# Second mixture: two arms behind 256 unbranched columns instead of seven widths, and one copy of the last tile's halves per expert

## The chip, the core and the metric

The kernel runs on one core of one Trainium2 chip. The metric is the device time of one execution in microseconds (us), lower is better. The core has five engines that run their own instruction streams and wait for each other through semaphores: TensorE (PE; its weight loads are shown apart as PEld), VectorE (DVE), ScalarE (ACT), GpSimd (POOL) and SyncE (SP), which issues most of the DMA transfers. SBUF is the working memory, PSUM the memory into which TensorE writes its products.

## The reference, cut to what matters

Attention without a softmax feeds a dense block, and that feeds a mixture of eight experts ("the second mixture"), which is the part that the change touches. Each of 2,304 tokens goes to one expert; an expert takes at most `capacity` = 576 tokens.

```python
for i in range(N):                       # N = 2304
    e = expert_idx[i]
    if counts[e] < capacity:             # capacity = 576
        disp[e, counts[e]] = x[i]
        pos[i] = counts[e]; counts[e] += 1; keep[i] = True
h = np.maximum(np.einsum('ecd,edf->ecf', disp, w1), 0.0)   # 512 -> 1024, per expert
y = np.einsum('ecf,efd->ecd', h, w2)                       # 1024 -> 512
for i in range(N):
    if keep[i]:
        out[i] = gate_w[i] * y[expert_idx[i], pos[i]]
```

With the input of this case the experts are handled in an order that gives token counts of 625 (cut to 576), 167, 219, 614 (cut to 576), 160, 391, 76 and 52. The numbers can't be known when the program is built: the kernel reads them into registers and branches on them.

## The kernel before

Every f32 operand is split into a high and a low half (type f32r), and a product of two such operands is made of three products on TensorE (`PASSES`). For one expert the first matrix, w1, is taken in eight slices `f` of 128 rows of the hidden layer (`NF2` = 8). `part(e, f, h, o, w)` is one slice over `w` token columns: 12 products (4 chunks of the depth by 3 passes) into one PSUM tile. `hb` holds three such tiles of two banks each, and slice `f` uses tile `(8e + f) % 3`, so a slice waits for the readers of the third slice before it. `put_g` reads the tile over all 576 columns, whatever the expert's count is: ACT writes the high half of the rectified value to `g2[f][:, 0]`, then DVE the low half to `g2[f][:, 1]`.

How many columns TensorE computes is chosen on the chip: `widths` is a tree of branches on TensorE alone, with seven arms, 256, 304, 352, 400, 448, 512 and 576 columns (`LEVELS`). Each arm has its own code, so slice `f` holds 6 x 12 + 24 = 96 products in its program, of which 12 or 24 run. All experts but the first are unrolled in this way: `up2(e, i)` holds two slices, under a branch of all engines on whether the expert has over 128 tokens. An expert with at most 128 takes the other side of that branch, `turned`, where the tokens are the stationary operand: 12 products of 256 columns for two slices, a copy by ACT, and two transposes.

A slice of 576 columns does not fit in one bank, so that arm starts in the middle of the first bank, and ACT and DVE read from a register offset, `off[e]`, which is 0 or 256.

After the up part comes `down(e, t)`, one tile of 128 tokens at a time: `whole` with three passes, or, for a tile with at most 64 tokens, `half`, whose stationary operand `gl` holds high and low halves of 64 tokens side by side. `gl[f]` is copied out of `g2[f]` on ACT by `put_last`, once for each slice, at the column `last[e]`.

The instructions of each engine run in the order in which the program is written (`manual_schedule`). Around the up part ACT and POOL also split the weights that come in by DMA (`next_pair`: two casts on ACT, two subtractions on POOL for each pair of tiles), ten pairs ahead of their use. A pair's stage buffer is one of four; SP issues the next load when POOL has released one, and the loads of the next expert's tokens (`load_x`, tile `xr`) stand in the same queue.

Of the kernel before, what the change touches and what calls it, by code (L numbers as in the profile page):

```python
# [19 lines left out]
P = 128  # L20
# [6 lines left out]
def attn_moe_kernel(ctx: ExitStack, tc: tile.TileContext, cap, kp, vp, qt, gn, wm, wg, wgt, w1, w2, ident, tri, out):  # L27
# [28 lines left out]
    tri_sb = const.tile([P, 2, P], BF16, name="tri_sb")  # L56
    cnt = const.tile([P, E], F32, name="cnt")
    cnt_i = const.tile([P, E], I32, name="cnt_i")
    off_i = const.tile([P, E], I32, name="off_i")
    last_i = const.tile([P, E], I32, name="last_i")  # L60

    ek_i = const.tile([P, E], I32, name="ek_i")
# [460 lines left out]

    LAG, LEAD = 2, 4
    HOT = 9
    LEVELS = (NARROW, 304, 352, 400, 448, BANK, cap)
    units = []

    with tc.manual_schedule(engines={mybir.EngineType.SP}):
# [189 lines left out]
        v.tensor_scalar(cnt, cnt, 1.0, -1.0, op0=ALU.max, op1=ALU.add)  # L719
        v.tensor_copy(last_i, cnt)  # L720
        v.tensor_scalar(last_i, last_i, 7, 7, op0=ALU.logical_shift_right, op1=ALU.logical_shift_left)
        v.tensor_scalar(off_i, cnt, float(BANK - 1), float(BANK - NARROW), op0=ALU.is_gt, op1=ALU.mult)
    ph1.close()


# [7 lines left out]
    psum = [ctx.enter_context(tc.tile_pool(name=f"psum{i}", bufs=1, space=PSUM)) for i in range(2)]  # L733
    hb = [psum[0].tile([P, 2 * BANK], F32, name=f"hb{i}") for i in range(3)]
    bk = [psum[1].tile([P, 512], F32, name=f"bk{i}") for i in range(2)]
    g2 = [g2_p.tile([P, 2, cap], F32R, name=f"g2_{f}") for f in range(NF2)]

    gl = [g2_p.tile([P, 2, HALF], F32R, name=f"gl_{f}") for f in range(NF2)]
    x2 = x2_p.tile([P, 2, KD, cap], F32R, name="x2")
    meta = {}  # L740

# [16 lines left out]
    with tc.manual_schedule():  # L758
# [44 lines left out]
        def part(e, f, h, o, w, x=x2):  # L803


            order = [(c, a, m) for c in range(KD) for a, m in PASSES]
            if f == 0:
                order = [(c, a, m) for a, m in ((0, 0), (1, 0), (0, 1)) for c in range(KD)]
            for k, (c, a, m) in enumerate(order):
                nc.tensor.matmul(  # L810
                    h, lhsT=w1_at(e, f // 2, a, c)[:, f % 2 * P:(f % 2 + 1) * P], rhs=x[:, m, c, o:o + w],
                    start=k == 0, stop=k == 3 * KD - 1,
                )

        def widths(e, levels, arm):

            mid = len(levels) // 2
            if not mid:
                return arm(levels[0])
            with tc.If(n[e] > levels[mid - 1]) as c:  # L820
                widths(e, levels[mid:], arm)
            with c.Else():
                widths(e, levels[:mid], arm)

        def up(e, f):

            h = hb[(e * NF2 + f) % 3]

            def arm(w):
                if w > BANK:  # L830
                    part(e, f, h[:, BANK - NARROW:BANK], 0, NARROW)
                    part(e, f, h[:, BANK:BANK + w - NARROW], NARROW, w - NARROW)
                else:
                    part(e, f, h[:, :w], 0, w)

            widths(e, LEVELS, arm)
            put_g(f, h[:, bass.ds(off[e], cap)], slice(0, cap))

        turned_sb = [ht_p.tile([P, 2 * P], F32, name=f"turned{i}") for i in range(2)]

# [10 lines left out]
        def up2(e, i):  # L851

            with tc.If(nall[e] > P) as many:  # L853
                up(e, 2 * i)
                up(e, 2 * i + 1)
            with many.Else():
                if i == 0:
                    nc.scalar.copy(turned_sb[0], turned(e, 0))
                if i + 1 < NF2 // 2:
                    s = turned(e, i + 1)  # L860
                hs = [hb[(e * NF2 + 2 * i + k) % 3][:, :P] for k in range(2)]
                for k, h in enumerate(hs):
                    nc.tensor.transpose(h, turned_sb[i % 2][:, k * P:(k + 1) * P], id_sb)
                if i + 1 < NF2 // 2:
                    nc.scalar.copy(turned_sb[(i + 1) % 2], s)
                for k, h in enumerate(hs):
                    put_g(2 * i + k, h, slice(0, P))
            for f in range(2 * i, 2 * i + 2):
                put_last(f, bass.ds(last[e], HALF))

        def put_g(f, src, cols):

            g = g2[f][:, :, cols]
            nc.scalar.activation(out=g[:, 0], in_=src, func=AF.Relu)  # L874
            nc.vector.scalar_tensor_tensor(  # L875
                out=g[:, 1], in0=src, scalar=0.0, in1=f32(g[:, 0]), op0=ALU.max, op1=ALU.subtract
            )

        def put_last(f, cols):
            nc.scalar.copy(gl[f], f32(g2[f][:, :, cols]))  # L880

        def up_rest(f):

            h = hb[f % 3][:, BANK:]
            with tc.If(n[0] > BANK) as wide:
                part(0, f, h[:, :cap - NARROW], NARROW, cap - NARROW)
            with wide.Else():
                with tc.If(n[0] > NARROW) as some:
                    part(0, f, h[:, :BANK - NARROW], NARROW, BANK - NARROW)
                with some.Else():  # L890
                    nothing(h, P)
            put_g(f, h[:, :cap - NARROW], slice(NARROW, cap))
            put_last(f, bass.ds(last[0], HALF))

        def down(e, t):
            w = rows(t)

            ps = hb[((e + 1) * NF2 + t + (e + 1 < E)) % 3][:, :BANK] if t < 2 else bk[t % 2]

            m = meta[e]  # L900
            o = ypool.tile([P, ROW], F32, tag="y", name="o")

            def products(lhs, passes):
                k, n = lhs(0, 0).shape[1], 0
                for f in range(NF2):
                    for a, b in passes:
                        nc.tensor.matmul(  # L907
                            ps[:k, :], lhsT=lhs(f, a), rhs=we2[e, f][:, b, :],
                            start=n == 0, stop=n == len(passes) * NF2 - 1,
                        )  # L910
                        n += 1

            def whole():
                products(lambda f, a: g2[f][:, a, t * P:t * P + w], PASSES)
                nc.scalar.activation(out=o[:w, :DM], in_=ps[:w, :], func=AF.Copy, scale=m[:w, t, 0:1])
                scatter("out", out, m[:w, t, 1:2].bitcast(I32), o[:w, :DM], NTOK - 1)

            def half():

                products(lambda f, a: gl[f].rearrange("p a t -> p (a t)"), ((0, 0), (0, 1)))  # L920
                g = m[:HALF, t, 0:1]
                nc.scalar.activation(out=o[:HALF, :DM], in_=ps[:HALF, :], func=AF.Copy, scale=g)  # L922
                nc.vector.scalar_tensor_tensor(  # L923
                    out=o[:HALF, :DM], in0=ps[HALF:, :], scalar=g, in1=o[:HALF, :DM], op0=ALU.mult, op1=ALU.add
                )
                scatter("out", out, m[:HALF, t, 1:2].bitcast(I32), o[:HALF, :DM], NTOK - 1)

            if w <= HALF:
                half()
            else:  # L930
                with tc.If(nall[e] > t * P + HALF) as more:  # L931
                    whole()
                with more.Else():
                    half()
# [17 lines left out]
        for f in range(3):  # L952
# [13 lines left out]
            skip_runtime_bounds_check_because="the counts are clamped to the capacity on the chip",  # L966
        )

        _, off = nc.values_load_multi_w_load_instructions(
            off_i[0:1, :], engines=[ET.Activation, ET.DVE], min_val=0, max_val=BANK - NARROW,  # L970
            skip_runtime_bounds_check_because="the offsets are one of two numbers",
        )

        _, last = nc.values_load_multi_w_load_instructions(
            last_i[0:1, :], engines=[ET.Activation], min_val=0, max_val=(cap - 1) // P * P,
            skip_runtime_bounds_check_because="the counts are clamped to the capacity on the chip",
# [11 lines left out]
        for e in range(E):  # L988
            if e + 1 < E:
                for t in range(4):  # L990
                    load_x(e + 1, t)
            if e == 0:
                with tc.If(early > NARROW - 1) as done:
                    for f in range(NF2):
                        up_rest(f)
                with done.Else():
                    tr_x(0, 0)
                    tr_x(0, 1)
                    for f in range(NF2):
                        up(0, f)  # L1000
                        put_last(f, bass.ds(last[0], HALF))
            else:
                for i in range(NF2 // 2):
                    up2(e, i)
                    if i < NF2 // 2 - 1:
                        next_pair((AP, AP))
            if e + 1 < E:
                tr_x(e + 1, 0)
                tr_x(e + 1, 1)
                for t in range(4, NST):  # L1010
                    load_x(e + 1, t)
            if e:
                next_pair((AP, AP))
            next_pair((AP, AP))
            next_pair((AP, AP))
            down(e, 0)
            if e + 1 < E:
                rest_x(e + 1, range(2, NST))
            with tc.If(nall[e] > P) as some:  # L1019
                down(e, 1)  # L1020
            with some.Else():
                nothing(hb[((e + 1) * NF2 + 2) % 3], P)
            next_pair((AP, AP))
            next_pair((AP, AP))
            down_rest(e, 2)
# [50 lines left out]
```

## Time and profile before

| What | Value |
|---|---|
| time of the runs, median of 3 | 810.14 us (810.14 to 811.97) |
| time of the profiled execution | 804.85 us |
| its span, first to last instruction | 803.1 us |
| mean granted TensorE clock, share of full speed | 0.968 |
| TensorE busy | 729.3 us, 91% of the span |
| ScalarE, VectorE, GpSimd busy | 310.5, 371.1, 291.5 us |
| second mixture, from the products of the first expert on | about 486 to 803 us of the span |

The profile is one execution. Starts and windows count from the first instruction. A row of the timeline merges instructions that follow each other; the brackets at its end give the idle time before it and the event that came last before it, which the profile infers and which is not always the true cause. [...] "issue" is idle time in which the engine waited for nothing that the profile shows.

### The profile page before, as it was taken

The numbers are of one execution on the slowest core, as the hardware profiler recorded it, in microseconds if no ns is written. First come the engines' busy times: TensorE is split into PE (matmuls) and PEld (weight loads), VectorE is DVE, ScalarE is ACT, GpSimd is POOL, SyncE is SP. The second block draws the span as 40 slices with busy tenths as digits, with TensorE's granted clock in tenths as the row PEclk, the third lists the DMA queues.
The fourth block names the chain that finished last, engine by engine and source line by source line (L and its number), as shares of the span: only waits on it lengthen the run. The fifth ranks groups of instructions, "written<-read, shape, count | busy, mean of one in ns | idle before, by whom it ended". The sixth has DMA issues, their size and how long they took to land. (4 is left out here: it accounts for less than half of the span.)

```text
span 803.1 us, 12019 instructions
## 1 busy us (share of the span) xinstructions
PE 729.3 (91%) x3988; PEld 648.0 (81%) x3988; DVE 371.1 (46%) x829; ACT 310.5 (39%) x650; POOL 291.5 (36%) x288
## 2 busy tenths in 40 slices
PE   6788999999999999999999899997879997879663
PEld 6777999989999998899989788876768976777553
DVE  2999767279924943494469434202212202221101
ACT  2555454242223322322334533424635444544422
POOL 2575233030212002102104923253847373667440
PEclk9899999999999999999999999999969999999779
DMA  9937898020212012001004723353444454455400
GB/s 332 373 123 275 290 302 292 27 76 1 105 69 77 1 66 83 27 1 53 13 1 158 233 97 106 100 165 109 143 164 148 165 154 136 129 182 164 152 20 11
DMA packets 38044, 102.82 MB, mean 128 GB/s; under 512 B 4451, under 2 KB 4707, under 8 KB 37920
## 3 DMA queue, kind: packets, MB, share of 16 engines
q1 hardware_dynamic: 34912, 91.99, 35.0%
q0 software_dynamic: 3008, 9.10, 3.0%
q8 instruction: 87, 1.43, 0.8%
q14 instruction: 37, 0.30, 0.1%
HBM read 77.78 MB, written 23.91 MB: 127 GB/s over the span
## 5 line engine op out<-in xcount | busy, mean ns | idle before, releaser
L273 PE MATMUL pk<-xT,w 128*128 128x384 f32 x1152 | 223.1, 341 | 7.5 <-POOL w L183 4.6
L292 PE MATMUL pk<-w,g 128*128 128x512 f32 x864 | 218.3, 394 | 2.5 <-ACT g L284 2.5
L273 PEld LDWEIGHTS pk<-xT,w 128*128 128x128 f32 x1152 | 201.6, 188 | 17.3 <-POOL w L183 5.9
L194 POOL TENSOR_TENSOR w<-st,w 128x512 fp32r<-128x512 f32 x128 | 161.2, 1294 | 120.2 <-ACT w L190 120.2
L292 PEld LDWEIGHTS pk<-w,g 128*128 128x128 f32 x864 | 160.2, 188 | 31.7 <-ACT g L284 3.1
L810 PE MATMUL hb<-x,w 128*128 128x256 f32 (+2 forms) x672 | 105.5, 316 | 24.5 <-issue 11.3
L810 PEld LDWEIGHTS hb<-x,w 128*128 128x128 f32 x672 | 99.4, 203 | 29.9 <-issue 14.4
L875 DVE SCALAR_TENSOR_TENSOR g<-hb,g 128x576 fp32r<-128x576 f32 (+3 forms) x72 | 41.4, 586 | 147.6 <-ACT g L874 147.6
L281 ACT ACTIVATE rr<-pk 128x384 f32<-128x384 f32 x96 | 47.1, 491 | 154.2 <-PE pk L273 154.0
L283 DVE TENSOR_TENSOR pk<-pk,rr 128x384 f32<-128x384 f32 x96 | 54.0, 563 | 75.0 <-ACT rr L281 74.2
L102 POOL DMA_INDIRECT disp<-y,sli x18 | 19.0, 1058 | 173.5 <-DVE sli L409 52.9
L354 DVE SCALAR_TENSOR_TENSOR junk<-y,wgb 128x512 f32<-128x512 f32 x120 | 77.9, 684 | 0.6 <-ACT y L312 0.6
L190 ACT CAST w<-st 128x512 fp32r<-128x512 f32 x128 | 71.5, 620 | 11.6 <-DMA st<-in_w 11.2
L284 ACT CAST g<-pk 128x384 fp32r<-128x384 f32 x96 | 46.0, 479 | 72.2 <-DVE pk L283 71.8
L285 DVE TENSOR_TENSOR g<-pk,g 128x384 fp32r<-128x384 f32 x96 | 53.3, 556 | 36.3 <-ACT g L284 36.1
L183 POOL TENSOR_TENSOR w<-cf,w 128x512 fp32r<-128x512 f32 x32 | 46.8, 1481 | 61.4 <-ACT w L182 56.8
L907 PE MATMUL hb<-w,g 128*128 128x512 f32 x264 | 65.8, 407 | 3.2 <-DVEq L946 2.9
L907 PEld LDWEIGHTS hb<-w,g 128*128 128x128 f32 x264 | 50.2, 194 | 15.3 <-DVEq L946 3.2
L874 ACT ACTIVATE g<-hb 128x576 fp32r (+3 forms) x72 | 36.1, 515 | 66.3 <-PE hb L810 63.4
L102 POOL DMA_INDIRECT out<-o,meta x22 | 21.3, 968 | 56.5 <-DVEq L1019 22.6
L923 DVE SCALAR_TENSOR_TENSOR o<-bk,meta,o 64x512 f32<-64x512 f32 x3 | 2.3, 751 | 70.5 <-ACT o L922 50.6
L239 POOL TENSOR_SCALAR ms<-ss 128x8 f32<-128x8 f32 x18 | 4.6, 253 | 76.2 <-DVE ss L237 75.9
(134 smaller groups left out, 651.6 us busy)
## 6 DMA issues: line engine op xcount, KB each, us to landing
st<-in_w SPq DMA_DIRECT2D x64, 512.0 KB, 3.9
st<-in_wm SPq DMA_DIRECT2D x32, 512.0 KB, 6.9
disp<-zrow SPq DMA_DIRECT2D x9, 1028.0 KB, 11.2
xr<-disp SPq DMA_DIRECT2D x32, 257.0 KB, 4.8
k<-in_kp SPq DMA_DIRECT2D x16, 320.0 KB, 4.4
v<-in_vp SPq DMA_DIRECT2D x16, 320.0 KB, 4.1
q<-in_qt SPq DMA_DIRECT2D x18, 256.0 KB, 3.2
out<-zrow SPq DMA_DIRECT2D x9, 512.0 KB, 8.3
```

Source lines behind the costliest of these rows:

```text
L183: nc.gpsimd.tensor_tensor(w[:, 1, :], o, f32(w[:, 0, :]), op=ALU.subtract)
L190: nc.scalar.copy(w[:, 0, :], s[:, i, :])
L194: e.tensor_tensor(w[:, 1, :], s[:, i, :], f32(w[:, 0, :]), op=ALU.subtract)
L273: nc.tensor.matmul(h, lhsT=wi[f][:, a, c * P:(c + 1) * P], rhs=xT[j][:, m, c, :], start=n == 0, stop=n == 3 * KD - 1,)
L281: nc.scalar.activation(out=r, in_=h, func=AF.Relu)
L283: nc.vector.tensor_tensor(h, h, r, op=ALU.mult)
L284: nc.scalar.copy(g[:, 0, :], h)
L285: nc.vector.tensor_tensor(g[:, 1, :], h, f32(g[:, 0, :]), op=ALU.subtract)
L292: nc.tensor.matmul(ysets[j == 1][i], lhsT=g[:, a, i * P:(i + 1) * P], rhs=wo[f][:, m, :], start=f == 0 and n == 0, stop=f == NF - 1 and n ...
L354: nc.vector.scalar_tensor_tensor(out=junk, in0=yt[j * TB + i][:, :DM], scalar=1.0, in1=wgb[e // 2][:, e % 2, :], op0=ALU.mult, op1=ALU.mul ...
L810: nc.tensor.matmul(h, lhsT=w1_at(e, f // 2, a, c)[:, f % 2 * P:(f % 2 + 1) * P], rhs=x[:, m, c, o:o + w], start=k == 0, stop=k == 3 * KD - 1,)
L907: nc.tensor.matmul(ps[:k, :], lhsT=lhs(f, a), rhs=we2[e, f][:, b, :], start=n == 0, stop=n == len(passes) * NF2 - 1,)
```

## The change

A slice first computes 256 columns without any branch. Then one branch asks whether the expert has more than 256 tokens; if so, a second one picks an arm of 160 more columns (to 416) or of 320 more (to 576); if not, TensorE does one tiny product (`nothing`, 8 columns). All slices now start in the middle of the first bank, so `off` and its register loads go. `gl` is written once for each expert, by one ACT copy behind the eight slices, and for that the `g2` tiles become slices of one tile.

```diff
-    LEVELS = (NARROW, 304, 352, 400, 448, BANK, cap)
+    MIDDLE = 416
...
-        v.tensor_scalar(off_i, cnt, float(BANK - 1), float(BANK - NARROW), op0=ALU.is_gt, op1=ALU.mult)
...
-    g2 = [g2_p.tile([P, 2, cap], F32R, name=f"g2_{f}") for f in range(NF2)]
-
-    gl = [g2_p.tile([P, 2, HALF], F32R, name=f"gl_{f}") for f in range(NF2)]
+    g2_all = g2_p.tile([P, NF2, 2, cap], F32R, name="g2")
+    g2 = [g2_all[:, f] for f in range(NF2)]
+
+    gl = g2_p.tile([P, NF2, 2, HALF], F32R, name="gl")
...
-        def widths(e, levels, arm):
-
-            mid = len(levels) // 2
-            if not mid:
-                return arm(levels[0])
-            with tc.If(n[e] > levels[mid - 1]) as c:
-                widths(e, levels[mid:], arm)
-            with c.Else():
-                widths(e, levels[:mid], arm)
-
         def up(e, f):
 
-            h = hb[(e * NF2 + f) % 3]
-
-            def arm(w):
-                if w > BANK:
-                    part(e, f, h[:, BANK - NARROW:BANK], 0, NARROW)
-                    part(e, f, h[:, BANK:BANK + w - NARROW], NARROW, w - NARROW)
-                else:
-                    part(e, f, h[:, :w], 0, w)
-
-            widths(e, LEVELS, arm)
-            put_g(f, h[:, bass.ds(off[e], cap)], slice(0, cap))
+            h = hb[(e * NF2 + f) % 3][:, BANK - NARROW:]
+            part(e, f, h[:, :NARROW], 0, NARROW)
+            with tc.If(n[e] > NARROW) as more:
+                with tc.If(n[e] <= MIDDLE) as some:
+                    part(e, f, h[:, NARROW:MIDDLE], NARROW, MIDDLE - NARROW)
+                with some.Else():
+                    part(e, f, h[:, NARROW:cap], NARROW, cap - NARROW)
+            with more.Else():
+                nothing(h[:, NARROW:], P)
+            put_g(f, h[:, :cap], slice(0, cap))
...
-            for f in range(2 * i, 2 * i + 2):
-                put_last(f, bass.ds(last[e], HALF))
...
-        def put_last(f, cols):
-            nc.scalar.copy(gl[f], f32(g2[f][:, :, cols]))
...
-                products(lambda f, a: gl[f].rearrange("p a t -> p (a t)"), ((0, 0), (0, 1)))
+                products(lambda f, a: gl[:, f].rearrange("p a t -> p (a t)"), ((0, 0), (0, 1)))
...
-        _, off = nc.values_load_multi_w_load_instructions(
...
                 for i in range(NF2 // 2):
                     up2(e, i)
                     if i < NF2 // 2 - 1:
                         next_pair((AP, AP))
+            nc.scalar.copy(gl, f32(g2_all[:, :, :, bass.ds(last[e], HALF)]))
             if e + 1 < E:
                 tr_x(e + 1, 0)
                 tr_x(e + 1, 1)
```

The order of TensorE's instructions at a slice of the second expert shows how much code stands between the products that run. Before, these are the last 12 of the slice's 18 rows: the arms of 448, 400, 352, 304 and 256 columns, behind those of 576 and 512 (`hb` is the PSUM tile, `x` the tokens, `w` the weights; an x12 is one `part`).

```order
L820 COMPARE_AND_BRANCH
L810 MATMUL hb_4470<-x_4489,w 128x448 x12
L820 UNCONDITIONAL_BRANCH
L810 MATMUL hb_4470<-x_4489,w 128x400 x12
L820 UNCONDITIONAL_BRANCH
L820 COMPARE_AND_BRANCH x2
L810 MATMUL hb_4470<-x_4489,w 128x352 x12
L820 UNCONDITIONAL_BRANCH
L810 MATMUL hb_4470<-x_4489,w 128x304 x12
L820 UNCONDITIONAL_BRANCH
L810 MATMUL hb_4470<-x_4489,w 128x256 x12
L820 UNCONDITIONAL_BRANCH
```

With the change the whole slice is these rows:

```order
L809 MATMUL hb_4468<-x_4473,w 128x256 x12
L818 COMPARE_AND_BRANCH
L819 COMPARE_AND_BRANCH
L809 MATMUL hb_4468<-x_4473,w 128x160 x12
L819 UNCONDITIONAL_BRANCH
L809 MATMUL hb_4468<-x_4473,w 128x320 x12
L819 UNCONDITIONAL_BRANCH
L777 LDWEIGHTS tri_sb
L777 MATMUL hb_4468<-tri_sb 128x8
L818 UNCONDITIONAL_BRANCH
```

The 256 columns moved from the far end of the slice to its front, and a slice holds 37 products in place of 96. The second place is ScalarE behind the last two slices of an expert (`g_6`, `g_7` are the `g2` tiles, `gl` the halves, the first CAST pair splits the next expert's tokens, `w<-st` the weights). Before:

```order
L787 UNCONDITIONAL_BRANCH x2
L880 ISA
L880 COPY gl_4487<-g_6_4479 128x128
L880 ISA
L880 COPY gl_4488<-g_7_4480 128x128
L794 CAST x_4489<-bk_4471 128x4x128
L794 CAST x_4489<-bk_4472 128x4x128
L190 CAST w<-st 128x512 x6
```

With the change:

```order
L786 UNCONDITIONAL_BRANCH x2
L983 ISA
L983 COPY gl<-g_4471 128x1024
L793 CAST x_4473<-bk_4469 128x4x128
L793 CAST x_4473<-bk_4470 128x4x128
L189 CAST w<-st 128x512 x6
```

One copy of 1,024 columns stands where the last two of 128 stood, and the six copies further up are gone.

## Rows read from the trace of the kernel before

**Rows 1.** Windows, up parts: busy us per engine (instructions), PEclk, DMA share, GB/s.

```profile
544.80:565.20 20.40, 15.10 (x106) 13.80 (x104) 6.05 (x8) 10.25 (x22) 8.72 (x9) 0.92 0.22 64
574.70:602.20 27.50, 19.66 (x107) 18.30 (x106) 5.97 (x8) 12.50 (x26) 15.41 (x15) 0.69 0.54 173
614.98:641.40 26.42, 26.42 (x201) 26.42 (x201) 5.30 (x7) 12.46 (x26) 13.88 (x13) 1.00 0.48 158
667.80:689.40 21.60, 13.72 (x105) 12.63 (x105) 6.06 (x8) 10.31 (x22) 8.69 (x9) 1.00 0.28 82
699.90:723.80 23.90, 19.60 (x103) 17.60 (x103) 6.82 (x9) 12.79 (x27) 15.09 (x17) 1.00 0.59 177
745.40:764.50 19.10, 10.24 (x62) 9.06 (x62) 4.00 (x11) 10.91 (x33) 9.78 (x10) 0.74 0.41 136
775.60:790.90 15.30, 8.82 (x56) 7.96 (x57) 1.46 (x6) 4.11 (x17) 0.00 (x0) 0.90 0.03 6
```

**Rows 2.** Timeline of TensorE, expert of 160: start, us, instructions, idle before.

```profile
667.87 3.15 PE L810 MATMUL hb<-x,w 128*128 128x256 f32 x24
672.73 3.10 PE L810 MATMUL hb<-x,w 128*128 128x256 f32 x24 [1.72 <-DVE g L875]
...
687.09 1.70 PE L810 MATMUL hb<-x,w 128*128 128x256 f32 x12 [2.19 <-DVE g L875]
688.62 1.04 PE L789 MATMUL bk<-id_sb,xr 128*128 128x128 f32 x8
```

**Rows 3.** The same stretch of the timeline, VectorE.

```profile
671.73 0.76 DVE L875 SCALAR_TENSOR_TENSOR g<-hb,g 128x576 fp32r<-128x576 f32 x1 [0.74 <-ACT g L874]
```

**Rows 4.** Timeline of TensorE, expert of 614.

```profile
614.94 0.18 PE L778 MATMUL hb<-tri_sb 128*128 128x8 bf16 x1
614.98 25.82 PE L810 MATMUL hb<-x,w 128*128 128x256 f32 x192
```

**Rows 5.** DMA queue of instructions, 667.8 to 689.4: packets, MB, share.

```profile
q8 instruction: 6, 0.10, 1.9%
```

**Rows 6.** Timeline, expert of 219: TensorE, and SP's loads of tokens.

```profile
588.31 2.93 PE L810 MATMUL hb<-x,w 128*128 128x256 f32 x12 [2.70 <-issue]
...
583.39 1.97 SPq L750 DMA_DIRECT2D xr<-disp  x4
```

**Rows 7.** The page's DMA issues: count, KB each, median us to landing.

```profile
xr<-disp SPq DMA_DIRECT2D x32, 257.0 KB, 4.8
```

**Rows 8.** Timeline of TensorE: runs of products without a gap, by width.

```profile
7.68 1.35 PE L209 MATMUL pk<-v,k 128*128 128x128 f32 x10 [0.30 <-DMA v<-in_vp]
...
481.23 1.00 PE L332 MATMUL pk<-wg_raw,yT 128*128 128x8 f32 x8
...
492.33 5.99 PE L810 MATMUL hb<-x2e,w 128*128 128x256 f32 x48
...
715.17 6.96 PE L810 MATMUL hb<-x,w 128*128 128x400 f32 x36 [1.37 <-issue]
```

**Rows 9.** Timeline of TensorE, last expert (52 tokens).

```profile
775.60 2.90 PE L846 MATMUL hb<-w,x 128*128 128x256 f32 x12 [3.49 <-issue]
...
782.61 1.66 PE L846 MATMUL bk<-w,x 128*128 128x256 f32 x12 [2.34 <-issue]
...
790.49 0.41 PE L863 MATMUL hb<-id_sb,turned 128*128 128x128 f32 x2 [2.85 <-issue]
790.93 3.99 PE L907 MATMUL hb<-w,gl 128*128 128x512 f32 x16
```

**Rows 10.** The same end, ScalarE.

```profile
790.82 0.45 ACT L874 ACTIVATE g<-hb 128x128 fp32r<-128x128 f32 x2 [1.97 <-PE hb L863]
791.46 0.50 ACT L880 CAST gl<-g 128x128 fp32r x2 [0.19 <-DVE g L875]
```

**Rows 11.** Groups by line: count, busy us, mean ns, idle before.

```profile
L190 ACT CAST w<-st 128x512 fp32r<-128x512 f32 x128 | 71.5, 620 | 11.6 <-DMA st<-in_w 11.2 <-PE pk L292 0.4
L880 ACT CAST gl<-g 128x128 fp32r x64 | 18.1, 295 | 18.8 <-DVE g L875 18.8
L194 POOL TENSOR_TENSOR w<-st,w 128x512 fp32r<-128x512 f32 x128 | 161.2, 1294 | 120.2 <-ACT w L190 120.2
```

More of the change, by code (lines that the diff above doesn't have):

```diff
@@ L58, in attn_moe_kernel @@
     cnt_i = const.tile([P, E], I32, name="cnt_i")
-    off_i = const.tile([P, E], I32, name="off_i")
     last_i = const.tile([P, E], I32, name="last_i")
@@ L892, in up_rest @@
             put_g(f, h[:, :cap - NARROW], slice(NARROW, cap))
-            put_last(f, bass.ds(last[0], HALF))
         def down(e, t):
@@ L967, in attn_moe_kernel @@
         )
-        _, off = nc.values_load_multi_w_load_instructions(
-            off_i[0:1, :], engines=[ET.Activation, ET.DVE], min_val=0, max_val=BANK - NARROW,
-            skip_runtime_bounds_check_because="the offsets are one of two numbers",
-        )
         _, last = nc.values_load_multi_w_load_instructions(
@@ L1000, in attn_moe_kernel @@
                         up(0, f)
-                        put_last(f, bass.ds(last[0], HALF))
             else:
```

## The prediction

> **What bounds the kernel now.** I read the up parts of the second mixture expert by expert, first as windows, then as a timeline of TensorE alone. The windows stand in the order of the experts with 167, 219, 614, 160, 391, 76 and 52 tokens [rows 1]. The reader should compare the first column with TensorE's busy time. For 614 tokens they are equal, 26.42 us: TensorE is the limit. For 167, 219 and 160 tokens, which run the same 256-column arm, TensorE is idle for 5.3, 7.8 and 7.9 us, and no other engine is near full (ACT at most 12.5, DVE 6.1, POOL 15.4 us). For 391 tokens 4.3 us are idle, for 76 and 52 tokens 8.9 and 6.5.
>
> The timeline shows where: two slices of the 160-token expert run back to back in 3.10 us, and between pairs or single slices stand gaps, here of 1.72 and 2.19 us [rows 2]. The bracket names DVE, and this is the trap. The gap of 1.72 us ends at 672.73 just after DVE's work on slice 1 [rows 3], but the slice that starts there is slice 2, whose PSUM tile is another one and was last read before this expert began. So the gap is no wait for DVE. It is not the branch itself either: slices 2 and 3 have the same branches between them and no gap, and 614 tokens run 192 products in 25.82 us without one [rows 4]. What fits is the supply of instructions. The queue that loads them brought 6 packets of together 0.10 MB, some 16 KB each, in this stretch, one per 3.6 us [rows 5]. A 256-column slice uses 12 of its 96 products and jumps over the rest, so it runs through its code faster than packets arrive; a slice of 614 tokens takes 3.2 us of work and gives them time. [...]
>
> **The change, part by part.** *Narrow experts (167, 219, 160).* The code of a slice shrinks from 96 products to 37, so an up part should need some 3 packets; at 3.6 us each that is 10.8 us. TensorE's own work is 8 slices of 12 products at 5.99 us / 48 = 0.125 us [rows 8], 12.0 us; 8 tiny products that are new, at 0.04 to 0.18 us [rows 4], I take 0.1, 0.8 us; 8 transposes, 1.04 us [rows 2]. That is 13.8 us, more than the packets need, so TensorE becomes the limit. Against 20.4, 27.5 and 21.6 us [rows 1] this gives 6.6 + 13.7 + 7.8 = 28.1 us. In the 219-token expert the next tokens are loaded from 583.39 on and land some 4.8 us later [rows 6, 7], at 588.2, while the transposes would now be due at 574.7 + 12.8 = 587.5; they become what is late next. For that and for gaps that remain I take off 3 us: **25 us**.
>
> *The expert of 391.* Its 400-column arm, 6.96 us / 36 = 0.193 us a product, becomes 256 and 160 columns. No row has f32r products under 256 columns. From below: a straight line through 256 and 400 columns gives 0.080 us at 160. From above: a plain f32 product of 128 columns stands as two records, five of them take 1.35 us, 0.27 us each [rows 8], or 0.34 us for 160 columns. Nearest are the records that carry a full set of weights over few columns: 8 columns take 1.00 us / 8 = 0.125 [rows 8], 128-column transposes 1.04 / 8 = 0.13 [rows 2]. There is a floor, and 256 columns already sit on it; I take 0.125. So a slice costs 12 x 0.25 = 3.0 us, eight 24.0 us, with 4 transposes (0.5) 24.5 against 23.9 now: **-0.6 us**; the bounds are 4.3 us better and 12 x 8 x 0.215 = 20.6 us worse.
>
> [...]
>
> *The expert of 614 and the first one* run the same products as before and wait for nothing but TensorE: 0.
>
> *The turned experts (76, 52).* Their own products stay, but they jump over two slices each time, now 74 products in place of 192. With the 14 products they run, a pair is 88 in place of 206. Idle are 8.9 + 6.5 us [rows 1], in gaps like those at 782.61 and 790.49 [rows 9]. They run through code still faster than narrow slices do, so not all goes: I take half, **7.7 us**, between 0 and 15.4.
>
> *The copies.* 64 copies of 0.295 us, 18.1 us of ACT, and 18.8 us of waiting for DVE [rows 11] become 8 copies. For 1,024 columns I go up the line from 128 columns (0.295) to 512 (0.620): 0.295 + 896 x 0.325 / 384 = 1.05 us. ACT's work in the windows leaves room, and the copy stands behind the last slice, where TensorE has transposes and 5 us of `down` before it needs ACT: the copy delays the split of the next tokens by under 1 us, covered. The cover is gone in one place. The last expert has at most 64 tokens, so its first tile is a `half` that needs `gl` at once. Before, it began at 790.93, since the early slices' halves lay ready; DVE's last slice ends and the copies start at about 791.5 to 791.6 [rows 9, 10], so now it begins near 791.65 + 1.05 = 792.7: **-1.8 us** at the very end of the kernel. The removed register loads and offsets stood in the shadow of early products: 0.
>
> **Sum.** 25 - 0.6 + 7.7 - 1.8 = 30.3 us. The profiled execution would go from 804.85 to 774.5 us. It was 5.3 us faster than the median of the runs, 810.14; against that median I predict **780 us**.
>
> **Rivals.** *B: fewer gaps, but each stays.* If a gap belongs to a packet's arrival and not to the pace, 7.9 us / 6 = 1.3 us per packet, three packets leave 3.9 us in each narrow expert: 28.1 - 11.7 = 16.4 in place of 25, so 789 us. For it: every slice still jumps. Against it: the 614-token expert took 7 packets' worth of time without a gap.
>
> *C: 160 columns at the price of plain f32.* 20.6 us worse, 801 us. For it speaks that no shorter f32r product stands anywhere; against it that each record of plain f32 takes the same 0.135 us as the floor, and an f32r product is one record.
>
> *D, the other side: the gaps belong to the branches.* Then they stay as they are. The narrow experts pay 24 tiny products, 2.4 us, the expert of 391 keeps 4.3 us of gaps on 24.5 us of work, 28.8 against 23.9, 4.9 us, and the last copy costs 1.8: 9.1 us slower, 819 us. It decides as soon as less than 9 us of the 41 us of gaps goes. [...]
>
> *E: gaps shrink by just what the rest costs*, no change: a quarter of the gaps gone, 9 to 10 us, for which no row speaks.
>
> **Chances.** My sum 0.57, B 0.20, C 0.12, D 0.06, E 0.05. The likeliest lies within 772 to 786. The range takes the low ends of the sum (all 28.1 us, a cheap 160, more of the turned gaps) and goes up to C: 768 to 800. A measurement here can tell 0.3%, 2.4 us, from no change: faster by more 0.89, within 0.05, slower by more 0.06.
>
> **What would show it.** In the windows of 167, 219 and 160 tokens the length should fall to 14 to 15 us with TensorE's busy time close to it and the granted clock at 1.00; instruction packets per expert should fall to about 3. Gaps of over 1 us between slices with as many packets gone would be B, as many gaps as now D. The 160-column products should stand about 0.125 us apart; 0.3 us would be C. The last `half` should begin about 1.8 us behind the last transposes. I would be wrong above all if gaps are set by what a jump costs and not by how much code lies behind it.

## The result, and the profile after

The changed kernel takes 764.78 us, median of 4 runs (761.26 to 768.74); the kernel before, on the same chip, 811.06 us (810.14 to 815.64). The ratio is 0.942, 95% interval 0.936 to 0.948: faster, and below the range of the prediction, 768 to 800 us. The profiled execution took 765.28 us, span 763.4, so from one profiled execution to the other it is 39.6 us where the prediction had 30.3; by the medians it is 46.3 us.

The windows of the up parts after, in the order and with the columns of [rows 1] (167, 219, 614, 160, 391, 76 and 52 tokens):

```profile
545.00:558.20 13.20, 13.20 (x113) 12.78 (x111) 6.06 (x8) 8.69 (x15) 8.47 (x8) 1.00 0.32 92
567.70:583.60 15.90, 13.74 (x113) 13.01 (x113) 6.72 (x9) 12.20 (x21) 15.41 (x14) 1.00 0.74 227
596.90:623.30 26.40, 26.40 (x201) 26.40 (x201) 5.30 (x7) 10.95 (x19) 13.91 (x13) 1.00 0.45 150
649.80:663.00 13.20, 13.20 (x112) 12.80 (x111) 6.06 (x8) 8.69 (x15) 8.45 (x7) 1.00 0.31 96
673.50:696.30 22.80, 22.80 (x200) 22.79 (x199) 6.06 (x8) 10.68 (x19) 15.71 (x18) 1.00 0.64 203
717.10:728.70 11.60, 9.23 (x64) 7.84 (x63) 2.57 (x9) 6.58 (x19) 6.89 (x6) 0.88 0.62 196
738.70:749.70 11.00, 8.74 (x56) 8.15 (x56) 2.05 (x8) 4.14 (x13) 1.26 (x2) 0.84 0.06 20
```

In four of the seven, length and TensorE's busy time are now equal, and in the first five the granted clock, as a share of full speed, is 1.00. The experts of 167 and 160 tokens went from 20.4 and 21.6 us to 13.2, the one of 219 from 27.5 to 15.9. Its missing 2.1 us are the wait that was named ahead, for the next tokens. The timeline of TensorE there, at the end of the up part:

```profile
580.36 0.18 PE L777 MATMUL hb<-tri_sb 128*128 128x8 bf16 x1
582.21 0.63 PE L788 MATMUL bk<-id_sb,xr 128*128 128x128 f32 x4 [1.67 <-DMA xr<-disp]
583.26 0.63 PE L788 MATMUL bk<-id_sb,xr 128*128 128x128 f32 x4 [0.43 <-DMA xr<-disp]
```

In the expert of 160 tokens [rows 2] one slice now follows the other, every 1.56 us, with the tiny product between them and no idle time. The same view, two of its slices:

```profile
651.27 1.69 PE L809 MATMUL hb<-x,w 128*128 128x256 f32 x12
652.79 0.18 PE L777 MATMUL hb<-tri_sb 128*128 128x8 bf16 x1
652.83 1.69 PE L809 MATMUL hb<-x,w 128*128 128x256 f32 x12
```

The turned experts kept some gaps, far fewer than before [rows 1, 9]. TensorE in the expert of 76 tokens, and in the last one, where the half waits for the one copy:

```profile
722.20 0.38 PE L851 MATMUL hb<-id_sb,turned 128*128 128x128 f32 x2
724.57 1.73 PE L834 MATMUL bk<-w,x 128*128 128x256 f32 x12 [2.00 <-ACT w L189]
...
738.71 2.15 PE L834 MATMUL hb<-w,x 128*128 128x256 f32 x12 [2.29 <-issue]
740.65 2.66 PE L834 MATMUL bk<-w,x 128*128 128x256 f32 x12
...
747.62 0.33 PE L851 MATMUL hb<-id_sb,turned 128*128 128x128 f32 x1 [0.16 <-DVE g L861]
```

The 2.00 us booked to ACT's weight split are no wait for weights: the split runs ten pairs ahead, and in the run with the least code (below) the same 12 products start without a gap.

The wait of the half is 1.77 us. Its 16 products then took 5.54 us at a granted clock of 0.69, where they had taken 3.99 at 1.00 [rows 9]. The whole row is in the timeline of all engines, with the copy ahead of it:

```profile
748.62 1.04 ACT L983 CAST gl<-g 128x1024 fp32r x1 [0.36 <-DVE g L861]
...
749.72 5.54 PE L889 MATMUL hb<-w,gl 128*128 128x512 f32 x16 [1.77 <-ACT gl L983]
```

The queue that loads instructions carried 87 packets, 1.43 MB, over the whole execution before and 59 after, by the two pages:

```profile
q8 instruction: 87, 1.43, 0.8%
```

```profile
q8 instruction: 59, 0.97, 0.5%
```

### The profile page after: what moved, and what is told of

Same layout as the page of the kernel before. It is cut to its first block, busy times and chain, and to the rows that moved or that the text cites. A ratio compares the mean times of both kernels' runs of the same rounds, so it can differ in the third digit from the quotient of the medians.

```text
span 763.4 us, 12001 instructions
## 1 busy us (share of the span) xinstructions
PE 723.3 (95%) x4108; PEld 646.4 (85%) x4108; DVE 370.7 (49%) x828; ACT 302.1 (40%) x594; POOL 291.6 (38%) x288
## 4 chain that ended last, share of the span: by engine, by line
PE 71%; DMA 14%; POOL 5%; issue 4%; DVE 3%; ACT 1%; SPq 1%; POOLq 0%
PE pk L272 23%; PE pk L291 22%; PE hb L809 11%; DMA out<-o,meta 11%; PE hb L889 6%; PE bk L889 4%; POOL w L193 2%; PE pk L226 1%; PE pk L208 1%; POOL r L240 1%; POOL w L182 1%; DMA k<-in_kp 1%; DMA q<-in_qt 1%; PE bk L788 1%; DMA xr<-disp 1%
## 5 line engine op out<-in xcount | busy, mean ns | idle before, releaser
L809 PE MATMUL hb<-x,w 128*128 128x256 f32 (+2 forms) x768 | 100.2, 290 | 0.1
L101 POOL DMA_INDIRECT disp<-y,sli x18 | 19.1, 1059 | 173.1 <-DVE sli L408 52.9
L860 ACT ACTIVATE g<-hb 128x576 fp32r<-128x576 f32 (+3 forms) x72 | 36.3, 517 | 57.1 <-PE hb L809 39.5
```

Source lines behind the costliest of these rows:

```text
L809: nc.tensor.matmul(h, lhsT=w1_at(e, f // 2, a, c)[:, f % 2 * P:(f % 2 + 1) * P], rhs=x[:, m, c, o:o + w], start=k == 0, stop=k == 3 * KD - 1,)
```

## The experiments

Below, "idle of the turned experts" is the length of their two up parts, from first to last product, less TensorE's busy time in them, from windows cut there: 12.4 us before, 2.9 after. The expert of 76 tokens before (the one of 52 stands in [rows 1]), then both after:

```profile
745.40:761.00 15.60, 9.69 (x59) 8.77 (x60) 2.22 (x8) 7.60 (x25) 6.57 (x6) 0.80 0.44 144
```

```profile
717.10:727.80 10.70, 8.33 (x59) 7.19 (x59) 2.22 (x7) 5.90 (x17) 6.00 (x6) 0.92 0.61 203
738.70:748.00 9.30, 8.74 (x56) 8.15 (x56) 1.66 (x7) 2.83 (x12) 1.26 (x2) 0.82 0.07 24
```

The packets of instructions are those of the whole execution. The median of the kernel before varied from 804.8 to 811.1 us between the sets of runs, so ratios are what compares.

**The two parts apart.** First the copy alone:

```diff
-            for f in range(2 * i, 2 * i + 2):
-                put_last(f, bass.ds(last[e], HALF))
...
+            nc.scalar.copy(gl, f32(g2_all[:, :, :, bass.ds(last[e], HALF)]))
```

> The kernel before with one part of the change alone: the halves of the last tile are copied once per expert, the seven widths stay. Supply theory (TensorE's gaps come from the code that it must load when it jumps over much of it): the code is as long as before, so the gaps stay; only the last expert's half comes about 2 us later, a ratio to before of 1.00 to 1.005, windows of 160 and 167 tokens 20 to 22 us. Copy theory (the 64 copies on ACT and the waits behind them held TensorE up): the gaps go without the shorter code, ratio 0.95 to 0.96.

Measured: 814.84 us, ratio 1.0095 (1.0063 to 1.0127), 87 packets, gaps as before: the expert of 160 tokens takes 22.2 us, of which TensorE works 16.2. The copies did not hold TensorE up. That it lost 1% and not 0.5% can be read for the most part from the end of its profile: the last expert's up part took 16.9 us, 15.3 before; the half waited 1.77 us for the copy; and the first 12 of its 16 products took 4.65 us in place of 3.05, the granted clock of the last of the page's 40 slices at 0.6 in place of 0.9. Together that is 5.0 of the 6.7 us between the medians.

Then the arms alone, the copies left slice by slice:

```diff
+            for f in range(2 * i, 2 * i + 2):
+                put_last(e, f)
...
-            nc.scalar.copy(gl, f32(g2_all[:, :, :, bass.ds(last[e], HALF)]))
```

> The other part alone: 256 columns without a branch and two arms past them, the halves copied slice by slice as before. Supply theory: all of the gain is here, 763 to 767 us, and the last half waits less for its copy, so up to 2 us better than the whole change. Copy theory: little gain, 795 us or more.

Measured: 761.96 us, ratio 0.9439 (0.9385 to 0.9493). All of the gain is in the arms; with the copies left in, ACT's 64 copies wait 18.9 us for DVE as before, and the kernel is no slower.

**Code that never runs.** First with a condition that always holds:

```diff
-                    part(e, f, h[:, NARROW:cap], NARROW, cap - NARROW)
+                    with tc.If(n[e] <= cap) as real:
+                        part(e, f, h[:, NARROW:cap], NARROW, cap - NARROW)
+                    with real.Else():
+                        for _ in range(5):
+                            part(e, f, h[:, NARROW:cap], NARROW, cap - NARROW)
```

> The changed kernel with code that never runs added on the side past 256 columns, so that a slice has 97 products of code again and not 37. Experts of up to 256 tokens take the very same branches and run the same instructions; they only jump further. Supply theory: the gaps come back, up parts of 160, 167 and 219 tokens 19 to 27 us in place of 13 to 16, 76 and 52 tokens 15 to 19 in place of 11 to 12, the whole 30 to 40 us slower than the changed kernel. Branch theory (fewer branches made the gain): these windows stay within 0.5 us; only experts past 256 tokens pay one more branch.

The second had `range(2)`.

> The same with less dead code, 61 products of code a slice. If the pace of loading decides (one packet per 3.1 to 3.6 us, and an expert needs its whole code in packets): some 4 packets or 14 us in an expert of up to 256 tokens, which hides almost all, 0 to 3 us slower in all, the turned experts a few us worse. If the distance of a jump decides (a target that is not loaded yet costs 1 to 3 us each time): the turned experts, which jump over 122 products in place of 74, lose most of what they won, 8 to 13 us, and the others some. Branch theory: no change.

Measured: 762.59 and 760.77 us, ratios 0.9436 (0.938 to 0.9492) and 0.9408 (0.9356 to 0.9461), the time of the changed kernel. They say nothing on the theories: the count is declared to be at most `cap`, so the condition can be decided when the program is built, and with 59 packets in both, as in the changed kernel, no code seems to have been added. What they give is, as far as TensorE goes, the changed kernel's time twice more: medians of 761 to 765 us. The edit again, with a condition that only the chip can decide, and whose other arm no expert here takes:

```diff
+                    with tc.If(n[e] > MIDDLE + 4) as real:
+                        part(e, f, h[:, NARROW:cap], NARROW, cap - NARROW)
+                    with real.Else():
+                        for _ in range(5):
+                            part(e, f, h[:, NARROW:cap], NARROW, cap - NARROW)
```

> What the run with 97 products was meant to be: there the condition was one that the compiler can decide, and the code that never runs was not in the program. Now the condition is that an expert has more than 420 tokens, and the arm with 60 more products a slice is in it. Experts of up to 256 tokens run what they run in the changed kernel, with one branch, and jump over 85 products. Supply theory: the gaps come back, windows of 167, 219 and 160 tokens 19 to 27 us, 76 and 52 tokens 15 to 19 us, instruction packets back to 85 or more, the whole 795 to 810 us. Branch theory (the number of branches decides, two in a row before, one now): windows within 0.5 us of the changed kernel's, the whole 760 to 767 us.

Measured: 812.39 us, ratio to before 1.0063 (1.0029 to 1.0098), 2 us above what was expected. All that the change won is gone, by code that no expert runs. The packets are back:

```profile
q8 instruction: 85, 1.39, 0.7%
```

The windows of this run, experts of 167 and 160 tokens, and TensorE's timeline inside the latter:

```profile
544.20:567.30 23.10, 15.82 (x114) 14.50 (x113) 6.13 (x9) 8.94 (x15) 8.68 (x9) 0.93 0.23 70
...
667.40:686.30 18.90, 14.61 (x104) 13.54 (x103) 6.05 (x8) 8.32 (x14) 8.68 (x9) 0.91 0.24 71
```

```profile
670.57 1.67 PE L809 MATMUL hb<-x,w 128*128 128x256 f32 x12
673.54 0.18 PE L777 MATMUL hb<-tri_sb 128*128 128x8 bf16 x1 [1.29 <-issue]
673.66 1.67 PE L809 MATMUL hb<-x,w 128*128 128x256 f32 x12
676.72 0.18 PE L777 MATMUL hb<-tri_sb 128*128 128x8 bf16 x1 [1.39 <-issue]
```

The reader should see where the gap stands: between the 256-column products and the tiny product on which the jump lands; the bracket names no engine. The idle of the turned experts is 15.1 us:

```profile
747.70:763.10 15.40, 7.55 (x57) 6.82 (x58) 2.22 (x7) 6.15 (x18) 8.46 (x8) 1.00 0.52 169
773.20:791.90 18.70, 11.44 (x56) 10.12 (x56) 1.47 (x6) 2.65 (x11) 1.69 (x2) 0.73 0.05 14
```

With `range(2)`, 61 products of code a slice:

> The same with 24 products of code that never runs, 61 a slice. If the pace of loading decides: an expert of up to 256 tokens needs some 4 packets, 14 us at 3.6 us each, which its 13 us of work nearly hide: 0 to 3 us slower in those three together, the turned experts 3 to 6 us. If each jump past what is loaded costs 1 to 3 us: the turned experts lose 8 to 13 us and the others several us each. Branch theory: no change.

Measured: 772.24 us, ratio 0.9588 (0.9525 to 0.9652), 69 packets. The narrow experts hide it almost wholly, the first by the window with no idle time at all:

```profile
546.40:559.90 13.50, 13.50 (x114) 12.99 (x113) 6.13 (x9) 8.76 (x15) 8.66 (x9) 1.00 0.29 93
569.40:584.00 14.60, 13.89 (x115) 13.06 (x114) 6.19 (x9) 10.86 (x19) 14.12 (x13) 1.00 0.73 246
```

The turned experts don't: idle of 8.2 us, 5.3 more than after. Both as the pace of loading had it.

```profile
718.80:729.70 10.90, 7.59 (x60) 6.88 (x60) 2.22 (x7) 6.37 (x18) 6.83 (x6) 1.00 0.57 198
739.20:754.00 14.80, 9.92 (x56) 8.86 (x56) 1.47 (x6) 2.81 (x12) 2.30 (x3) 0.73 0.06 17
```

**Branches.** Two more in a row on the narrow way, with tiny products only:

```diff
             with more.Else():
-                nothing(h[:, NARROW:], P)
+                with tc.If(n[e] > 240) as one:
+                    nothing(h[:, NARROW:], P)
+                with one.Else():
+                    with tc.If(n[e] > 230) as two:
+                        nothing(h[:, NARROW:], P)
+                    with two.Else():
+                        nothing(h[:, NARROW:], P)
```

> The changed kernel with two more branches in a row on the way of experts of up to 256 tokens, each with one tiny product on either side, so hardly any code more. Supply theory: within 0.5 us of the changed kernel in each window. Branch theory: gaps of 1 to 2 us at half of the slices or more, as before, windows of 160 and 167 tokens 18 us or more.

Measured: 763.46 us, ratio 0.9467 (0.9423 to 0.9511). Two more branches in each slice of the narrow experts cost nothing that shows; the experts of 167 and 160 tokens:

```profile
542.50:555.90 13.40, 13.40 (x114) 12.96 (x113) 6.09 (x9) 8.76 (x15) 8.60 (x9) 1.00 0.31 94
646.70:660.10 13.40, 13.40 (x114) 12.96 (x113) 6.09 (x9) 8.76 (x15) 8.58 (x9) 1.00 0.30 95
```

And the kernel before with one branch less on that way, the code as long:

```diff
-            widths(e, LEVELS, arm)
+            with tc.If(n[e] > NARROW) as wide:
+                widths(e, LEVELS[1:], arm)
+            with wide.Else():
+                arm(NARROW)
```

> The kernel before with one thing changed: whether an expert has at most 256 tokens is asked first, by one branch, in place of two in a row. The code is as long as before, 96 products a slice, of which 84 are jumped over. Supply theory: as before, 160 and 167 tokens 20 to 22 us, ratio 1.00 within 0.01. Branch theory: the gaps of 160, 167 and 219 tokens go or halve, 10 to 20 us faster than before.

Measured: 807.69 us, ratio 0.9998 (0.9958 to 1.0038), 87 packets. The gaps stay where they were, and the brackets name ACT, DVE and "issue" in turn for the same kind of gap. TensorE, expert of 160 tokens:

```profile
671.28 3.15 PE L810 MATMUL hb<-x,w 128*128 128x256 f32 x24
675.90 3.11 PE L810 MATMUL hb<-x,w 128*128 128x256 f32 x24 [1.46 <-ACT gl L883]
680.02 1.69 PE L810 MATMUL hb<-x,w 128*128 128x256 f32 x12 [1.01 <-DVE g L878]
682.98 1.70 PE L810 MATMUL hb<-x,w 128*128 128x256 f32 x12 [1.26 <-issue]
```

**256 columns inside the arms.** The kernel before with three widths and the one copy:

```diff
-    LEVELS = (NARROW, 304, 352, 400, 448, BANK, cap)
+    LEVELS = (NARROW, 416, cap)
```

> The kernel before with three widths (256, 416, 576) behind branches in place of seven, and one copy per expert: as little code as with the change (36 + 12 products a slice), but the 256 columns stand inside the arms. Supply theory: the gaps go as they do with the change, up parts of 160 and 167 tokens 13 to 14 us, and the expert of 391, which runs one product of 416 columns in place of 256 and 160, takes about 19.5 us, 3 us less; the whole is 0 to 3 us faster than the changed kernel. If it is 256 columns ahead of every branch that closes the gaps (work in hand while the jump is served): gaps of 1 us or more stay and the whole is 10 us or more slower than the changed kernel.

Measured: 762.92 us, ratio 0.9415 (0.936 to 0.9469), 63 packets. So it need not be 256 columns ahead of the branch: less code is enough. The products of the expert of 391 take 19.1 us in place of 22.4, since 96 products of 416 columns take the place of 192; the longer code (48 products a slice) gives most of it back in the turned experts, whose idle is 5.6 us.

**One far jump in place of eight.** The dead code of 97 products a slice, all of it in an expert's first slice:

```diff
+                    if f:
+                        part(e, f, h[:, NARROW:cap], NARROW, cap - NARROW)
+                    else:
+                        with tc.If(n[e] > MIDDLE + 4) as real:
+                            part(e, f, h[:, NARROW:cap], NARROW, cap - NARROW)
+                        with real.Else():
+                            for _ in range(5 * NF2):
+                                part(e, f, h[:, NARROW:cap], NARROW, cap - NARROW)
```

> As much code that never runs as in the run with 60 products of it a slice, but in one block of 480 products in the first slice of an expert, so that it is jumped over once and not eight times. If the queue fetches what is jumped over as well (volume decides): packets back to 85, and each up part as long as there, the whole 795 to 812 us. If a far jump only costs its own fetch and the rest is left out: packets stay at 60 to 68, one gap of 1 to 3.5 us in each of seven experts, the whole 770 to 785 us.

Measured: 781.14 us, ratio 0.9712 (0.9659 to 0.9765), 70 packets, two more than the upper bound set for them: as much code, and some 30 us faster than in eight pieces. Each expert has a gap or two at the jump or soon behind it, together 1.0 to 3.7 us in the five that are not turned; those of 614 and 391 tokens, which had none, now have one. The packets by the page, and TensorE at the start of these two:

```profile
q8 instruction: 70, 1.15, 0.6%
```

```profile
600.08 3.44 PE L809 MATMUL hb<-x,w 128*128 128x256 f32 x24
606.08 24.16 PE L809 MATMUL hb<-x,w 128*128 128x256 f32 x168 [2.57 <-issue]
...
685.33 2.99 PE L809 MATMUL hb<-x,w 128*128 128x256 f32 x24
691.64 21.16 PE L809 MATMUL hb<-x,w 128*128 128x256 f32 x168 [3.31 <-issue]
```

**Less code still.** No middle arm, 25 products a slice, and the last copies in pairs (below):

```diff
-                with tc.If(n[e] <= MIDDLE) as some:
-                    part(e, f, h[:, NARROW:MIDDLE], NARROW, MIDDLE - NARROW)
-                with some.Else():
-                    part(e, f, h[:, NARROW:cap], NARROW, cap - NARROW)
+                part(e, f, h[:, NARROW:cap], NARROW, cap - NARROW)
```

> The run with the last copies in pairs, and without the arm up to 416 tokens: 25 products of code a slice in place of 37. The expert of 391 runs 256 and 320 columns, as the one of 614 does, 25.8 us in place of 22.4: 3.4 us slower. If volume of code decides, the turned experts, whose gaps are still 5 us, win 1.5 to 3 us: the whole 759 to 763 us, no better than with the arm. If their remaining gaps belong to the jumps and not to the code: 763.5 us or more.

Measured: 759.61 us, ratio 0.9422 (0.9386 to 0.9458), 53 packets. The expert of 391 lost its 3.5 us; the turned experts are idle for 2.1 us in all, windows from first to last product:

```profile
722.70:731.00 8.30, 7.57 (x60) 6.92 (x60) 2.22 (x7) 5.72 (x17) 4.26 (x4) 1.00 0.57 208
738.70:747.10 8.40, 7.03 (x57) 6.66 (x57) 1.47 (x6) 3.84 (x14) 5.18 (x5) 1.00 0.07 24
```

Against the run with the copies in pairs alone (760.05 us, below), loss and gain cancel.

**The price of few columns.** `MIDDLE = 392` and `MIDDLE = 512` in place of 416:

> The changed kernel with 136 columns in the middle arm in place of 160 (391 tokens still fit). Floor theory (an f32r product with weights of its own costs about 0.112 us however few its columns): the expert of 391 stays within 0.2 us of its 22.75 us. A straight line by columns: 96 products by 24 columns are 1 us shorter or more.

> The same with 256 columns in the middle arm. Floor theory: 96 products go from 0.112 to 0.122 us, the expert of 391 takes about 1 us more, 23.7 us. A straight line by columns through zero (0.070 us more at 256 than at 160, were 160 columns at 0.075): some 4 us more.

Measured: 763.88 and 762.79 us, ratios 0.943 (0.9375 to 0.9484) and 0.9422 (0.9367 to 0.9477), no difference from the changed kernel. The 192 products of the expert of 391 show the size; the changed kernel with 160 columns, then 136, then 256:

```profile
673.53 22.44 PE L809 MATMUL hb<-x,w 128*128 128x256 f32 x192
```

```profile
674.30 22.38 PE L809 MATMUL hb<-x,w 128*128 128x256 f32 x192
```

```profile
674.79 23.28 PE L809 MATMUL hb<-x,w 128*128 128x256 f32 x192
```

With 256 columns in both halves a product takes 23.28 / 192 = 0.121 us. So 96 of 160 columns take 22.44 - 11.64 = 10.80 us, 0.1125 each, and of 136 columns 0.112: the floor. (In the expectation for 256 columns, a line through zero from 0.075 us at 160 gives 0.045 us more and not 0.070; the 4 us that it leads to are right.)

**The last copy.** After each pair of slices, in the last expert alone:

```diff
+                    if e + 1 == E:
+                        pair = slice(2 * i, 2 * i + 2)
+                        nc.scalar.copy(gl[:, pair], f32(g2_all[:, pair, :, bass.ds(last[e], HALF)]))
...
-            nc.scalar.copy(gl, f32(g2_all[:, :, :, bass.ds(last[e], HALF)]))
+            if e + 1 < E:
+                nc.scalar.copy(gl, f32(g2_all[:, :, :, bass.ds(last[e], HALF)]))
```

> The changed kernel, but the last expert's halves are copied after each pair of slices, 256 columns each time, since nothing lies over that one copy. If the last copy is on the path that sets the end: the first half no longer waits 1.77 us for it, the whole is 1 to 1.8 us faster. If the wait only moves to the next thing that is late (the last slice's work on DVE and ACT): under 0.5 us.

Measured: 760.05 us (758.64 to 762.27, 6 runs), ratio 0.9376 (0.9335 to 0.9418), the lowest ratio of all runs. The wait is gone, and the half's products are back at 3.98 us from 5.54, so the trace shows some 3.3 us where 1 to 1.8 were expected; TensorE, the last transpose and the half:

```profile
747.88 0.33 PE L851 MATMUL hb<-id_sb,turned 128*128 128x128 f32 x1 [0.16 <-DVE g L861]
748.26 3.98 PE L889 MATMUL hb<-w,gl 128*128 128x512 f32 x16
```

Its interval still overlaps that of the changed kernel, so the total alone does not separate the two.

## Why the prediction missed

*The mechanism was right.* The gaps are the supply of TensorE's instructions and not DVE, ACT or the branches. Code that never runs brings them back (812 us), two more branches don't (763 us), one branch less with the code as long changes nothing (ratio 0.9998), and the copies are no part of it (1.0095). Rivals B and D fell: the narrow experts have no gap of that kind left, and fewer or more branches leave the time as it is. C fell by the floor, E by the result.

*The step that failed is the term for the turned experts, "I take half".* It gave 7.7 us, less 1.8 for the last copy, 5.9 net. Measured, from [rows 1] to the windows above: 7.5 us for 76 tokens, 4.3 for 52 with the copy's wait inside, and 1.2 from the gap ahead of the last expert, 3.49 us before [rows 9] and 2.29 after; 13.0 net. That is 7.1 of the 9.3 us by which the sum was short. In the prediction's own windows 4.6 of the 15.4 us of idle time remain, 1.8 of them the wait for the copy: some four fifths of the gaps went, not half. "Half" was not worked out from a row, though the packets were there to be used: three at 3.6 us, as for the narrow experts, give 10.8 us for each of the two, and they measured 11.6 and 11.0, the latter with the copy's 1.77 us inside, so that reckoning is good to a microsecond or two and no better. That these gaps follow the amount of code is shown over a range: 25, 37, 48, 61 and 97 products a slice left TensorE idle in the turned experts for 2.1, 2.9, 5.6, 8.2 and 15.1 us; the kernel before, with 96, for 12.4. Five more runs with 37 to 39 products lie at 2.6 to 3.1 by the gaps in their timelines (the changed kernel, so read, at 2.7), the one with the copies in pairs, which the run with 25 products has too, at 2.9. Had the 15.4 us been scaled by 37 / 96, 5.9 would have been left and 9.5 gone.

*Smaller ones.* The narrow experts gave 7.2 + 11.6 + 8.4 = 27.2 us where 25 was taken; the allowance of 3 us was for the wait for the next tokens, which came at the place named, 2.1 us, and for gaps that did not remain. The expert of 391 won 1.1 us in place of losing 0.6: the floor was the right idea, but 0.125 us a product is a little high, it is 0.121 at 256 columns and 0.1125 at 160. The last copy and its wait were sized right: 1.05 us estimated, 1.04 measured, 1.77 us of waiting for 1.8. Left out was the clock behind that wait: the half's products took 5.54 us in place of 3.99. These with the turned term make 11.0 us, 1.7 more than the 9.3, and the half's 1.55 us of lower clock are nearly all of the difference. The clock does not fall there every time: behind waits of 1.77 and 1.85 us the half took 4.0 us in the runs with 256 columns in the middle arm and with two more branches.

*The reference.* The sum, 774.5 us, was against a profiled execution 5.3 us faster than the median, and that difference was added to the forecast. After the change the profiled execution stood at the median (765.28 and 764.78), so these 5.3 us were no property of the kernel. The range's low end counted more of the turned gaps, but lay on this reference; against the profiled executions alone it would have held (768 less 5.3 is 762.7, below 765.28). So of the 14.7 us from the forecast to the profiled execution, 9.3 were the sum and 5.3 the reference.

*What a jump costs* was the doubt named last, and both sides are true in part. A jump far ahead has a price of its own: with one block, 1.0 to 3.7 us in an expert, in those with much work too (2.57 us at the jump in the expert of 614). With short jumps it is the amount that counts, against the work that hides its loading, since short jumps don't save the loading: 60 more products a slice in eight experts (the first holds its up part too, which it jumps over as a whole), 3,840 in all, brought 26 packets more, at 1.43 MB / 87 = 16.4 KB some 111 bytes a product; as one block they brought 11, under half. Jumps inside one expert's up part are not free either: with 97 products a slice, gaps of 1.29 and 1.39 us stand at jumps over 84 of them. From what length on a jump leaves a gap of its own, the runs do not settle: no run varied the length of a single jump in steps.

## What to carry to other kernels

Code that is branched over was not free here: 60 products a slice that no expert runs made 812 us of 765. On an engine that is the bound, count the products that stand in the program between those that run, and compare the packets of the instruction queue in a stretch, times the time of one (3.1 to 3.9 us in the windows of the kernel before in which TensorE waited), with the work in it. A finer choice of widths can cost more than the columns that it saves: seven arms lost some 45 us to the changed kernel's code, while 136, 160 or 256 columns in its middle arm made no difference that could be measured, nor did that arm itself. If rare code must stay, one block that is jumped over once is cheaper than a piece in every slice, here some 20 us in place of 50. A wait on the path can cost more than its length: behind the 1.77 us for the last copy, the lower clock took up to 1.55 us more.

## What was not expected of the hardware

The releaser that a timeline names for a gap of this kind means little: the same gaps are booked to DVE, ACT and "issue" in turn, in the run with the narrow way first within three rows (1.46, 1.01 and 1.26 us). And the expert of 614 tokens, which had no gap at its branches, waited 2.57 us at one jump over 480 products: the 3.4 us of products ahead of that jump did not hide it.
